# Two small gate loads moved from SyncE's queue to GpSimd's, and four warm-up products taken out

## The chip, the cores and the metric

The kernel runs on one core of a Trainium2 chip. The metric is the device time of one execution in microseconds, as the median of several runs. The profile is that of one execution, and its times count from the start of its span.

## The reference

Block attention whose keys and values are mixed by a normalised 8x8 matrix for each head, followed by a mixture of experts that sends each token to one of eight experts, with a bias by modality:

```
P = sort_net; five times: P = exp(P - rowmax); P /= rowsum; P /= colsum
k_sorted, v_sorted = einsum('bhij,bhjcd->bhicd', P, k_blocks / v_blocks)
attn = softmax(q_block @ k_sorted_block.T / 8);  x = attn @ v_sorted_block      # x: [3072, 512]
logits = x @ w_gate + modality_bias[modality_id];  e = argmax(logits)
out[token] = softmax(logits)[e] * (relu(x @ w1[e]) @ w2[e])
```

Shapes: q, k, v are 4x8x768x64, the sort matrices 4x8x8x8, w_gate 512x8, modality_bias 2x8, w1 8x512x1024, w2 8x1024x512, all float32; modality_id has 3072 entries.

## The kernel before, in words

The 32 (batch, head) pairs are worked in two groups of 16. A group's v (128 rows of 96 blocks' columns x 64) is loaded by four transfers (`load_v`, line 130), its k by three (`load_k`, line 134) and its q by four of 192 KB for each half (`load_q`, line 142). All of these cast float32 to bfloat16 and are issued by GpSimd (POOL), on the software queue. POOL carries out its instructions in the written order, computations and DMA issues in one line; `v_in` is the buffer of v, and is used again for k of the second group.

At the start, VectorE and ScalarE normalise P in five rounds (lines 248 to 281) while TensorE (PE) runs products on the identity whose results nobody reads (`spins`, line 234): ten, ten and eleven inside the rounds, and eight after `make_bd(0)`, which builds the mixing matrix `bd`. Then `sort_v` (line 301) mixes v, and `sort_k` (line 314) mixes k; each chunk of 16 or 64 products is copied out of PSUM by VectorE or ScalarE (lines 95, 97). A product of `sort_v` reads 128 columns of `v_in`, so all four transfers have to be there.

The gate's constants are small: `bias2` (the two bias rows, repeated on 128 partitions, 64 bytes each) and `wg_f` (w_gate, four runs of 32 bytes on each partition). `bias2` is first read by `rank_b` (lines 337 to 343, on POOL), from which `rank_c` (VectorE) derives `eI`, the two experts in use, A and B. `wg_f` is first read by `rank_e` (line 416, on POOL). After `rank_b` the written order of POOL is: `rank_d`, `rank_ok` (small computations), `load_w` for half of expert A's weights (line 430, its address from `eI`), `pads` (memsets, iotas), `load_q` of the second half, `rank_e`, `rank_pen`, `load_w` for the rest of A and all of B, and `load_v` of the second group. Each `load_w` moves 512 KB.

Then come units of attention (`scores`, `expo`, `av`), in which pieces of the experts (`mG` line 534, `mL1` line 566, `mL2` line 580) are run as tokens become ready. From unit 7 on, POOL copies the second group's v into `kv` in four pieces (`relay_v`, line 138), between which it loads the second group's k into the freed parts of `v_in`. After unit 15, PE mixes the second group's v from `kv` (`sort_v(1, ...)`, line 301 again), then k, and runs units 16 to 31 and the rest of the experts. Results leave by indirect DMAs on POOL (line 588).

Of the kernel before, what the change touches and what calls it, by code (L numbers as in the profile page):

```python
# [8 lines left out]
FP32 = mybir.dt.float32  # L9
# [15 lines left out]
def kernel(  # L25
# [13 lines left out]
    nc = tc.nc  # L39
# [5 lines left out]
    E = moe_w_gate.shape[1]  # L45
# [25 lines left out]
    singles = ctx.enter_context(tc.tile_pool(name="singles", bufs=1))  # L71
# [56 lines left out]
    def load_v(g, z, nz=4):  # L128
        cs = slice(z * BLK // nz, (z + 1) * BLK // nz)
        nc.gpsimd.dma_start(out=v_in[:, cs], in_=v_src[g * 128:(g + 1) * 128, cs])  # L130
# [10 lines left out]
    def load_q(g, z, r, hh):  # L141
        nc.gpsimd.dma_start(out=q_in[r][z][:, 4 * hh:4 * hh + 4],  # L142
                            in_=q[2 * g + r, 4 * hh:4 * hh + 4, z * 4 * BLK:(z + 1) * 4 * BLK]
                            .rearrange("h (p t) d -> p h (t d)", t=3))
# [4 lines left out]
    make_identity(nc, ident)  # L149
    load_v(0, 2)  # L150
    load_v(0, 3)

    mod_w = moe_modality_id.tensor.reshape(list(moe_modality_id.tensor.shape)).bitcast(I32).ap()
    modI = singles.tile([32, BLK, 2], I32)
    nc.sync.dma_start(out=modI, in_=bass.AP(tensor=mod_w.tensor, offset=mod_w.offset,
                                            ap=[[2 * BLK, 32], [2, BLK], [1, 2]]))
    bias2 = singles.tile([128, 2, E], FP32)
    nc.sync.dma_start(out=bias2, in_=bass.AP(tensor=moe_modality_bias.tensor, offset=moe_modality_bias.offset,
                                             ap=[[0, 128], [E, 2], [1, E]]))
    wg_f = singles.tile([128, 4, E], FP32)  # L160
    nc.sync.dma_start(out=wg_f, in_=moe_w_gate.rearrange("(c p) e -> p c e", p=128))

    maskUT = singles.tile([128, 128], BF16)
    make_upper_triangular(nc, maskUT, val=1.0, diag=False)
# [34 lines left out]
    for z in range(2):  # L199
        for r in range(2):  # L200
            load_q(0, 0, r, z)
    idI = singles.tile([BLK, 2, 32], I32)
    idm = singles.tile([BLK, 32 * 2 + 128], BF16)
    wgp = singles.tile([128, 2, 5, E + 1], BF16)
# [2 lines left out]
    def pads():  # L207
# [7 lines left out]
        for c in range(5):  # L215
# [7 lines left out]
                     ap=[P_t.ap[0], P_t.ap[2], P_t.ap[1]])  # L223
# [3 lines left out]
                   ap=[ident.ap[0], [1, NB], [NB, 16]])  # L227
# [4 lines left out]
    def spins(n):  # L232
        for _ in range(n):
            nc.tensor.matmul(spin[:, 0].rearrange("p (a b) -> p a b", a=4), ident, id4, start=True, stop=True)  # L234
# [50 lines left out]
    def make_bd(g):  # L285
        rep = ps(f"rep{g}")[:, 0, 0:64].rearrange("p (a b) -> p a b", a=NB)
        nc.tensor.matmul(rep.rearrange("p a b -> p (a b)"), sel[g].rearrange("p a b -> p (a b)"),
                         P_bf.rearrange("p a b -> p (a b)"), start=True, stop=True)
        rtmp = singles.tile([128, NB, NB], FP32, tag="rtmp", name=f"rtmp{g}")
        nc.vector.tensor_tensor(rtmp, rep, bc_mid(jmask, NB), ALU.mult)  # L290
        rr = singles.tile([128, NB], FP32, tag="rr", name=f"rr{g}")
        nc.vector.tensor_reduce(rr, rtmp, AX.X, ALU.add)
        bv = singles.tile([128, 16, NB], BF16, tag=f"bd{g}", name=f"bd{g}")
        (nc.gpsimd if g else nc.vector).tensor_tensor(bv, bmask.broadcast_to([128, 16, NB]), bc_mid(rr, 16), ALU.mult)
        bd.append(bv.rearrange("p a b -> p (a b)"))
# [39 lines left out]
    def rank_b():  # L335
        f_ = st["f"] = small("f_", 1)
        nc.gpsimd.tensor_scalar(f_, cumz[:, 32:33], float(HALF), None, ALU.is_le)
        d_ = small("d_", E)
        nc.gpsimd.tensor_tensor(d_, bias2[:, 1], bias2[:, 0], ALU.subtract)
        bAB = st["bAB"] = singles.tile([128, 2, E], FP32, tag="bAB", name="bAB")  # L340
        nc.gpsimd.tensor_scalar(d_, d_, f_, None, ALU.mult)
        nc.gpsimd.tensor_tensor(bAB[:, 0], bias2[:, 0], d_, ALU.add)
        nc.gpsimd.tensor_tensor(bAB[:, 1], bias2[:, 1], d_, ALU.subtract)
# [280 lines left out]
        return ran  # L624

    make_bd(0)
    spins(8)
    rank_b()
    sort_v(0, 0)
    sort_v(0, 1)  # L630
# [323 lines left out]
```

## Time and profile before

| | |
|---|---|
| median of 3 runs (lowest, highest) | 178.97 us (176.52 to 179.09) |
| the profiled execution: its own time; its span | 177.43 us; 175.8 us |
| PE, DVE, ACT, POOL busy | 158.5 (90%), 99.3 (57%), 96.5 (55%), 78.4 us (45%) |
| software queue (POOL) | 15664 packets, 19.93 MB |
| hardware queue (SyncE) | 768 packets, 0.06 MB |
| TensorE's granted clock, mean | 0.998 |

The span is what the profile shows of the execution; 1.6 us of the execution's own time lie outside of it. Busy time is a share of the whole span, and the stages have different limits, so the table says only that no engine but PE is near its full time; which wait sets the end is read from the rows.

### The profile page before, as it was taken

What the parts mean: (1) busy time and instruction counts of PE and PEld (TensorE: products, weight loads), DVE (VectorE), ACT (ScalarE), POOL (GpSimd) and SP (SyncE); (2) the same over time, 40 slices, a digit from 0 to 9 for tenths busy, and PEclk for the clock granted to TensorE, in tenths of its full rate; (3) what the DMA queues carried; (4) which work ended last, traced back from release to release, by engine and by line L of the source; (5) the groups of instructions that cost most, each with busy time, mean ns of one, the idle gap of its engine ahead of it and who ended that gap; (6) DMA issues with size and microseconds to landing.
All of it is one profiled execution on the core that took longest, in us unless ns stands there. A gap on an engine that the chain in (4) does not pass through costs nothing.

```text
span 175.8 us, 5331 instructions
## 1 busy us (share of the span) xinstructions
PE 158.5 (90%) x2248; PEld 114.9 (65%) x2248; DVE 99.3 (57%) x259; ACT 96.5 (55%) x151; POOL 78.4 (45%) x145
## 2 busy tenths in 40 slices
PE   2998997969999959889899999999999999999970
PEld 0346984758777548768585867867877666775730
DVE  3764966787765593847554667673765632322520
ACT  4212777765766548387556657768567532343220
POOL 7998698782205898982202222002222222242322
PEclk9999999999999999999999999999999999999999
DMA  3999999999999597999410303001100131112211
GB/s 41 154 213 217 197 202 201 122 174 199 207 211 212 137 174 124 172 210 189 101 63 7 117 0 121 4 0 65 60 28 35 63 121 60 60 63 81 98 69 64
DMA packets 16461, 20.37 MB, mean 116 GB/s; under 512 B 9999, under 2 KB 12079, under 8 KB 16432
## 3 DMA queue, kind: packets, MB, share of 16 engines
q0 software_dynamic: 15664, 19.93, 58.4%
q8 instruction: 18, 0.29, 0.7%
q1 hardware_dynamic: 768, 0.06, 0.4%
q14 instruction: 11, 0.09, 0.2%
HBM read 27.32 MB, written 6.55 MB: 193 GB/s over the span
## 4 chain that ended last, share of the span: by engine, by line
PE 54%; POOL 17%; DMA 12%; issue 7%; DVE 6%; POOLq 1%; ACT 0%; DVEq 0%
PE yp L580 19%; PE hp L566 18%; DMA v_in<-in_v_dram 10%; PE spin L234 6%; POOL kv L138 6%; DMA q_in<-in_q_dram 3%; POOL q_in L142 3%; PE ka L314 2%; PE sc L448 2%; PE op L468 2%; POOL out_dram L588 2%; PE lg L534 1%; DVE y L587 1%; DVE xb L473 1%; PE tq L324 1%
## 5 line engine op out<-in xcount | busy, mean ns | idle before, releaser
L588 POOL DMA_INDIRECT out_dram<-y,ids x25 | 25.1, 1002 | 76.7 <-ACT y L585 34.1
L580 PEld LDWEIGHTS <-hT 128*128 128x128 bf16 x200 | 18.3, 98 | 19.2
L454 ACT ACTIVATE attnT<-sc 96x768 bf16<-96x768 f32 x32 | 25.5, 806 | 9.4 <-PE sc L448 9.3
L554 ACT ACTIVATE hT<-hp 128x512 bf16<-128x512 f32 x37 | 21.8, 595 | 11.0 <-PE hp L566 8.5
L566 PE MATMUL hp<-XT,wB 128*128 128x256 bf16 (+1 forms) x224 | 24.9, 265 | 0.1
L580 PE MATMUL yp<-wB,hT 128*128 128x512 bf16 x104 | 24.3, 379 | 0.0
L587 DVE TENSOR_SCALAR y<-yp,gate 128x512 f32<-128x512 f32 x13 | 9.8, 750 | 24.2 <-PE yp L580 24.2
L566 PE MATMUL hp<-XT,wA 128*128 128x128 bf16 (+1 forms) x256 | 23.1, 246 | 0.3 <-DVE xb L473 0.2
L580 PE MATMUL yp<-wA,hT 128*128 128x512 bf16 x96 | 22.7, 380 | 0.0
L473 DVE TENSOR_TENSOR xb<-op,rs_all 96x512 bf16<-96x512 f32 x32 | 22.0, 687 | 1.1
L566 PEld LDWEIGHTS <-wB 128*128 128x128 bf16 x224 | 19.9, 98 | 3.0 <-DVE xb L473 0.2
L566 PEld LDWEIGHTS <-wA 128*128 128x128 bf16 x256 | 19.3, 97 | 2.1 <-DVE xb L473 0.4
L585 ACT ACTIVATE y<-yp,gate 128x512 f32<-128x512 f32 x12 | 8.3, 688 | 15.0 <-PE yp L580 15.0
L509 DVE CAST XT<-pm 128x720 f32 x16 | 14.5, 908 | 1.9 <-PE pm L499 0.8
L468 PEld LDWEIGHTS <-attnT 96*128 96x128 bf16 x256 | 11.8, 97 | 4.6 <-DVE xb L473 0.9
L472 DVE RECIPROCAL rs_all<-op 96x8 f32<-96x8 f32 x32 | 6.4, 199 | 14.0 <-PE op L468 13.7
L95 ACT CAST v_sb<-va 96x1024 bf16<-96x1024 f32 x11 | 10.7, 1012 | 6.5 <-PE va L301 6.4
L509 ACT CAST XT<-pm 128x720 f32 x16 | 12.3, 769 | 3.5 <-PE pm L499 2.1
L138 POOL COPY kv<-v_in 128x1536 bf16<-128x1536 bf16 x4 | 11.3, 2842 | 6.5 <-DMA v_in<-in_v_dram 6.5
L234 PE MATMUL spin<-ident 128*128 128x512 bf16 x39 | 11.1, 444 | 3.3 <-POOL ident masks.py:199 3.3
L468 PE MATMUL op<-v_sb,attnT 96*128 96x65 bf16 x256 | 13.0, 193 | 1.0 <-DVE xb L473 0.7
L555 DVE TENSOR_SCALAR hT<-hp 128x512 bf16<-128x512 f32 x13 | 8.9, 688 | 7.2 <-PE hp L566 7.1
(157 smaller groups left out, 222.9 us busy)
## 6 DMA issues: line engine op xcount, KB each, us to landing
v_in<-in_v_dram POOLq DMA_DIRECT2D x8, 384.0 KB, 13.7
q_in<-in_q_dram POOLq DMA_DIRECT2D x16, 192.0 KB, 7.4
wA<-in_moe_w_dram POOLq DMA_DIRECT2D x4, 512.0 KB, 8.1
wB<-in_moe_w_dram POOLq DMA_DIRECT2D x4, 512.0 KB, 12.9
kv<-in_k_dram POOLq DMA_DIRECT2D x3, 512.0 KB, 13.7
v_in<-in_k_dram POOLq DMA_DIRECT2D x3, 512.0 KB, 6.3
out_dram<-y,ids POOLq DMA_INDIRECT x25, 2.7
modI<-in_moe_modality_id_dram SPq DMA_DIRECT2D x1, 24.0 KB, 1.6
```

The lines of the kernel that those rows point to most:

```text
L95: nc.scalar.copy(dst, src)
L138: nc.gpsimd.tensor_copy(kv[:, 0:BLK * D].rearrange("p (d c) -> p d c", c=BLK)[:, :, cs], v_in[:, cs].rearrange("p c d -> p d c"))
L234: nc.tensor.matmul(spin[:, 0].rearrange("p (a b) -> p a b", a=4), ident, id4, start=True, stop=True)
L454: nc.scalar.activation(attnT[u % 2][:, 0:8 * BLK].rearrange("p (r f) -> p r f", r=2), sc_tiles.pop(u)[0:BLK, :, 0:4 * BLK], ACT.Exp, scale ...
L468: nc.tensor.matmul(op[:, r, j * (D + 1):(j + 1) * (D + 1)], attnT[u % 2][:, c0:c0 + 128], v_sb[0:BLK, r * 64 + (hh * 4 + j) * 8 + i, 0:D + ...
L473: nc.vector.tensor_tensor(xb[t % XB][:, :, hh * 256:(hh + 1) * 256].rearrange("p r (j d) -> p r j d", j=4), o4[:, :, :, 0:D], rs_all[:, u] ...
L509: ins = (nc.scalar.copy if side(t) == "act" else nc.vector.tensor_copy)(d, s_).ins
L554: return nc.scalar.activation(dst, src, ACT.Relu)
L566: mm = nc.tensor.matmul(hp[:, f], w1_t[m][:, c, fc * 128:(fc + 1) * 128], XT[:, c, row:row + n], start=(c == 0), stop=(c == 3))
L580: nc.tensor.matmul(yp, hT[s % 2][:, f, z * 128:(z + 1) * 128], w2_t[m][:, f], start=(f == 0), stop=(f == 7))
L587: nc.vector.tensor_scalar(y, yp, g_, None, ALU.mult)
L588: ins = nc.gpsimd.indirect_dma_start(out=out, out_offset=bass.IndirectOffsetOnAxis(ap=ids[:, k_:k_ + 1], axis=0), in_=y, in_offset=None, b ...
```

## The change

`bias2` is loaded by POOL right after the four transfers of v, and `wg_f` by POOL right after the four of the first half of q, where SyncE loaded both, third and fourth of its queue. The run of warm-up products behind `make_bd(0)` has four in place of eight. Nothing else differs; what is computed is the same.

```diff
     load_v(0, 2)
     load_v(0, 3)
+    bias2 = singles.tile([128, 2, E], FP32)
+    nc.gpsimd.dma_start(out=bias2, in_=bass.AP(tensor=moe_modality_bias.tensor, offset=moe_modality_bias.offset,
+                                               ap=[[0, 128], [E, 2], [1, E]]))
 
     mod_w = moe_modality_id.tensor.reshape(list(moe_modality_id.tensor.shape)).bitcast(I32).ap()
     modI = singles.tile([32, BLK, 2], I32)
     nc.sync.dma_start(out=modI, in_=bass.AP(tensor=mod_w.tensor, offset=mod_w.offset,
                                             ap=[[2 * BLK, 32], [2, BLK], [1, 2]]))
-    bias2 = singles.tile([128, 2, E], FP32)
-    nc.sync.dma_start(out=bias2, in_=bass.AP(tensor=moe_modality_bias.tensor, offset=moe_modality_bias.offset,
-                                             ap=[[0, 128], [E, 2], [1, E]]))
     wg_f = singles.tile([128, 4, E], FP32)
-    nc.sync.dma_start(out=wg_f, in_=moe_w_gate.rearrange("(c p) e -> p c e", p=128))
...
     for z in range(2):
         for r in range(2):
             load_q(0, 0, r, z)
+    nc.gpsimd.dma_start(out=wg_f, in_=moe_w_gate.rearrange("(c p) e -> p c e", p=128))
...
     make_bd(0)
-    spins(8)
+    spins(4)
     rank_b()
     sort_v(0, 0)
```

## Rows read from the trace of the kernel before

**Rows 1.** The page: busy tenths of PE in 40 slices of 4.4 us.

```profile
PE   2998997969999959889899999999999999999970
```

**Rows 2.** The chain that ended last, in order of time (start us, us).

```profile
37.62 16.82 DMA v_in<-in_v_dram
54.50 2.22 POOL kv L138
...
66.05 2.87 POOL kv L138
```

**Rows 3.** All engines in order of time, 65 to 81 us (start us, us).

```profile
69.23 1.23 PE L301 MATMUL va<-bd,kv 128*128 128x128 bf16 x16
```

**Rows 4.** POOL in order of time, first 38 us.

```profile
3.21 1.08 POOL L130 DMA_DIRECT2D v_in<-in_v_dram  x2
...
12.76 0.74 POOL L142 DMA_DIRECT2D q_in<-in_q_dram  x1 [0.29 <-DMA v_in<-in_v_dram]
13.58 0.25 POOL L337 TENSOR_SCALAR f__274<-cumz 128x1 f32<-128x1 f32 x1
...
14.79 0.21 POOL L343 TENSOR_TENSOR bAB<-bias,d__276 128x8 f32<-128x8 f32 x1
...
20.69 1.55 POOL L430 DMA_DIRECT2D wA<-in_moe_w_dram  x2 [1.23 <-issue]
...
24.83 3.02 POOL L142 DMA_DIRECT2D q_in<-in_q_dram  x4
...
32.97 1.59 POOL L430 DMA_DIRECT2D wA<-in_moe_w_dram  x2 [0.38 <-issue]
```

**Rows 5.** DMA in 40 slices, 28 to 38 us: GB/s.

```profile
GB/s 180 246 168 189 202 181 205 180 192 188 189 184 194 194 191 183 194 194 250 129 81 68 60 55 25 25 79 57 25 106 147 115 156 193 188 164 205 201 209 201
```

**Rows 6.** Line 130, landing of the v loads of 3.2 and 3.8 us.

```profile
DMA to landing us min/median/max: 9.3/9.3/9.3
...
DMA to landing us min/median/max: 9.3/9.9/10.6
```

**Rows 7.** All engines in order of time, 37 to 80 us.

```profile
39.22 0.54 POOL L130 DMA_DIRECT2D v_in<-in_v_dram  x1 [0.50 <-DMA wA<-in_moe_w_dram]
...
42.73 0.53 POOL L130 DMA_DIRECT2D v_in<-in_v_dram  x1 [2.97 <-DMA wA<-in_moe_w_dram]
...
48.41 1.91 PE L566 MATMUL hp<-XT,wB 128*128 128x256 bf16 x16
```

**Rows 8.** Line 430, landing: wA issued at 33.0, 33.8; wB at 34.8, 35.4.

```profile
DMA to landing us min/median/max: 6.0/7.3/8.6
...
DMA to landing us min/median/max: 10.2/11.1/12.0
```

**Rows 9.** DMA queues and issues, first 20 us (last column: us to landing).

```profile
q1 hardware_dynamic: 768, 0.06, 3.6%
...
wg_f<-in_moe_w_gate_dram SPq DMA_DIRECT2D x1, 16.0 KB, 9.5
```

**Rows 10.** PE in order of time, first 40 us.

```profile
3.32 4.45 PE L234 MATMUL spin<-ident 128*128 128x512 bf16 x10 [3.32 <-POOL ident masks.py:199]
...
12.70 1.90 PE L234 MATMUL spin<-ident 128*128 128x512 bf16 x8
14.47 1.63 PE L301 MATMUL va<-bd,v_in 128*128 128x128 bf16 x16
16.83 1.20 PE L314 MATMUL ka<-bd,kv 64*64 64x64 bf16 x64 [0.73 <-DMA kv<-in_k_dram]
...
39.06 0.48 PE L463 MATMUL op<-ident 128*128 128x252 bf16 x3 [1.27 <-ACT attnT L454]
```

**Rows 11.** SyncE's queue in order of time.

```profile
2.24 0.43 SPq L161 DMA_DIRECT2D wg_f<-in_moe_w_gate_dram  x1
```

**Rows 12.** DVE in order of time, first 40 us.

```profile
13.32 0.29 DVE L294 TENSOR_TENSOR bd<-bmask,rr 128x128 bf16<-128x128 f32 x1
...
17.28 0.15 DVE L347 TENSOR_REDUCE mxb<-bAB 128x2 f32<-128x16 f32 x1
```

## The prediction

> **What bounds the kernel now.** I read the slices of the page first: from the sixteenth on PE is busy for eight tenths or more in all but the last two [rows 1], so PE carries the second half, and what counts is when that half may begin. The chain of waits answers that: it runs through the landing of the second group's v at 54.44, the four copies of `relay_v` on POOL, the last of which ends at 66.05 + 2.87 = 68.92, and the first `sort_v` product of the second group [rows 2, 3]. That product starts at 69.23, with no wait shown on PE: PE arrived just then. The copies are early by some 0.25 us, no more.
>
> Going back from 54.44, the queue is full and in order, up to a hole: the rate falls from about 190 to 25 GB/s between 32.8 and 35.3 and then stays near 200 [rows 5]. What fills it again is the second half of expert A, issued by POOL at 32.97 [rows 4]; flow returns 1.5 to 2.3 us after that issue began. POOL had no stop between 12.76 and 32.97 that another engine ended: it computes, issues, computes; its 1.23 us before 20.69 are its own register work ("issue") [rows 4]. So **a microsecond added to POOL before 32.97 reaches the end**, less the 0.25 us.
>
> One wait of POOL matters for this change. The fourth q load stood 0.29 us for a transfer of v [rows 4]; the third v load had landed at 3.21 + 9.3 = 12.51 [rows 6]. Much later the third and fourth loads of the second v stood 0.50 and 2.97 us for wA [rows 7]; those landed at 33.0 + 6.0 = 39.0 and 33.8 + 8.6 = 42.4 [rows 8]. Count the software queue's transfers in written order: the 11th waits for the 3rd, the 26th for the 18th, the 27th for the 19th. Each waits for the one eight before; eight are in flight at most, and POOL stands still until there is room. (A limit on packets wouldn't fit: by the tiles' shapes 2,688 would be open in the first case, while the 25th transfer went through with 2,816.) SyncE's transfers don't enter this count.
>
> **The change part by part.**
>
> *Off SyncE's queue.* That queue's 768 packets take 3.6% of 16 engines over 20 us, 11.5 engine-us or 15 ns each [rows 9]; bias (128) and gate weights (512) are 640 of these, 0.60 us of every engine. They were in the way of v: wg_f was issued at 2.24 and landed 9.5 us later [rows 9, 11], ahead of the fourth v at 3.76 + 10.6 = 14.36 [rows 6]. The fourth v can come sooner by 0 (if the small packets fell into gaps) to 0.60; I take 0.5, since most of them ran beside a filled queue: **13.86**. SyncE's freed time serves nobody.
>
> *Four products fewer.* Eight took 1.90 us [rows 10], four end near 13.7; `bd` is ready at 13.61 [rows 12]. But in the profile `sort_v` starts at 14.47, right behind the landing of the fourth v, not behind the products. The cut alone is worth nothing to 0.1 us; with v earlier the start moves to about 13.9, 0.55 us sooner. PE is idle there for 0.2 us, or 0.8 if v doesn't come sooner. The products at the start show the lower level, 4.45 us for ten, and half of that later; after a gap of 1.27 us PE still ran at the upper one [rows 10] while the granted clock was 0.998 over the span. I charge nothing. The Trainium skill ("TensorE: Matmul & The Clock Gate", HAM oscillation) warns that a wait for data between products can drop the clock; that speaks against this part, and is a rival below.
>
> *Bias on POOL.* One more issue between v and k: as a v load of as many pieces, two of which took 1.08 [rows 4]; 0.55. It shifts k and the q loads. No cost by itself: v keeps the transfer engines busy until 13.86, and k was issued long before.
>
> *Gate weights on POOL.* One more issue behind the fourth q: 512 pieces like a q load, 0.74 to 0.76 us [rows 4]; 0.75.
>
> *The new waits.* With one more transfer in front, the fourth q is the 12th and waits for the 4th, the last v, instead of the third; the gate weights are the 13th and wait for the 5th, the bias. Before: landing 12.51, issue at 12.76, so 0.25 us to react. After: 13.86 + 0.25 = 14.11, q to 14.85, gate weights to 15.60. The bias, 0.12 us of packets behind v, has landed by then: no wait of its own. `rank_b` starts at 15.68, where it was at 13.58: **POOL is 2.1 us late**. Behind it stand `rank_c`, which VectorE began at 17.28 [rows 12] behind a v copy (`rank_b` took 1.42 us to 15.00 [rows 4], so its result now comes at 17.1: no stop), `load_w`, the second q, `rank_e`, and all later loads. wA's first half is issued at 22.8, into a queue that still holds q; its second half at 35.1. The hole grows by 2.1 us. The later pairs of the eight-in-flight rule keep their partners, both moved by two.
>
> A rule against this: the Trainium skill ("SBUF — State Buffer", SBUF: two separate sides) says that some VectorE copies lock GpSimd out, so that descriptors of its transfers can't be written, while SyncE's aren't touched. By that, the gate weights' issue could be held for one VectorE copy, an estimate of 1.2 us more. In this trace four q issues took 3.02 us beside VectorE's copies, 0.755 each, against 0.74 for the one alone [rows 4]: I add nothing.
>
> *Sum.* The last `relay_v` ends at 68.92 + 2.1 = 71.0. Does PE get there later still? Its weights land 2.1 later too: wB's first two at 35.4 + 12.0 + 2.1 = 49.5 [rows 8], where PE wanted them at 48.41 [rows 7] or sooner: 1.1 late, below 2.1, so the relays decide and the 0.55 us of the start is lost in them. End: 2.1 − 0.25 = 1.85, **+1.8 us**. Span 177.6, time 177.43 + 1.8 = 179.2 on the profiled execution's scale. The median of the runs is 1.54 higher, on its scale 180.8; the three runs spread over 2.6 us, and I predict the middle, **180.0**.
>
> Bounds: POOL's delay is 1.0 at least (0.55 + 0.75, less the 0.29 no longer waited: all issues, no new wait), and 3.8 at most (the bias landing only with the first k, at 16.8 less 0.5 [rows 10], then 0.25, 0.75 and 0.08 to 17.4). That is +0.75 to +3.6 us; less than nothing is excluded for POOL, since two issues are added to an engine that never rests there.
>
> **The rivals.** The times stand on the same middle scale, 178.2 plus the change. (1) *No new wait*: the limit of eight counts otherwise. POOL is 1.0 late: +0.75, 179.0. For it: three cases only. Against: they fit without remainder.
>
> (2) *The bias lands late*: small writes with a full k queue behind them report only when the slowest engine is through, at worst with the first k. Place: POOL's issue of the gate weights. It decides as soon as the bias lands after 14.6, one for one. At 16.3, +3.6 us: 181.8, slower by 2.0%. For it: wg_f took 9.5 us on its own queue [rows 9]. Against: that was beside v, and here 8 packets an engine stand behind v in order.
>
> (3) *The hole swallows the delay*: if the second q's tail, not the issue at 32.97, set the restart at 35.3, up to 1.7 us are free and the end is the same, 178.3. For it: rate was not zero in the hole [rows 5]. Against: at 25 GB/s most transfer engines had nothing left to do, and full rate came only after the new issue. More than this can't be won: the relays can't be earlier than POOL, so the 0.55 us at the start has no way to the end.
>
> (4) *The clock drops* in the gap before `sort_v`: the lower level lasted 4.45 us at the start and cost half of it, 2.2; PE would reach `sort_v(1)` later than the relays: +2.2, 180.4. The Trainium skill's page on the clock gate, named above, has this rule. Against: a 1.27 us gap without it.
>
> (5) *The change doesn't do what it says*: v doesn't come sooner. Then POOL is 2.6 late and the end +2.3, 180.5.
>
> **How the numbers follow.** Forecast 0.50, (5) 0.13, (1) 0.13, (2) 0.11, (3) 0.10, (4) 0.03. What a measurement of this kernel can tell from no change is about 2%, 3.6 us. Only (2), and (5) with a late bias, pass that: slower 0.14; faster 0.03 for what I don't see; the same 0.83. The range runs from 177.7 to 182.4: the hole case and the upper bound, each with some 0.6 us for the runs' own spread.
>
> **What would show it.** Right: the fourth q issue waits until the fourth v lands, near 14.1; gate weights issued near 14.9; `rank_b` near 15.7; wA's second half near 35.1; the hole longer by 2 us; the second v landing near 56.5; PE waiting before its first `va` of the second group, near 71. Wrong: `rank_b` before 14.7 (1), after 16.5 (2); a second v landing within 0.5 us of 54.44 (3); PE reaching `sort_v(1)` after POOL's last copy by over 0.5 us, which would make PE's own path the limit.

## The result and the profile after

| | before | after |
|---|---|---|
| median (lowest, highest) of 20 runs | 178.75 us (176.52 to 180.92) | 179.66 us (178.4 to 181.29) |
| the profiled execution: its own time; its span | 177.43; 175.8 us | 178.64; 177.0 us |
| TensorE's granted clock in it, mean | 0.998 | 0.981 |

Ratio 1.0066, 95% interval 1.0040 to 1.0091: 0.0066 of 178.75 is **+1.2 us**, the same as the difference of the two profiled spans; the medians differ by 0.9. Here and below medians are of all runs, while a ratio leaves out runs over 1.5% above the fastest of their kernel.

POOL in order of time, after (start us, us, what; in brackets the idle time before and who ended it):

```profile
3.21 1.09 POOL L130 DMA_DIRECT2D v_in<-in_v_dram  x2
4.28 0.56 POOL L153 DMA_DIRECT2D bias<-n_moe_modality_bias_dram  x1
...
10.72 3.02 POOL L142 DMA_DIRECT2D q_in<-in_q_dram  x4
14.60 0.76 POOL L201 DMA_DIRECT2D wg_f<-in_moe_w_gate_dram  x1 [0.85 <-DMA bias<-n_moe_modality_bias_dram]
15.43 0.24 POOL L337 TENSOR_SCALAR f__270<-cumz 128x1 f32<-128x1 f32 x1
...
34.78 1.60 POOL L430 DMA_DIRECT2D wA<-in_moe_w_dram  x2 [0.39 <-issue]
...
43.95 0.53 POOL L130 DMA_DIRECT2D v_in<-in_v_dram  x1 [2.73 <-DMA wA<-in_moe_w_dram]
```

The four q loads now go out without a stop; the wait stands one place later, before the gate weights, and it is for the bias. `rank_b` starts at 15.43 instead of 13.58 and wA's second half is issued at 34.78 instead of 32.97 [rows 4]: POOL is 1.85 and then 1.81 us late. The landings explain the two halves of this. Line 130's loads of 3.2 and 3.8 us, after:

```profile
DMA to landing us min/median/max: 6.9/7.7/8.5
```

So the third v is there at 3.21 + 6.9 = 10.1 and the fourth at 3.76 + 8.5 = 12.3, where they came at 12.51 and 14.36 [rows 6]. But the bias, issued half a microsecond behind the last v, is late. DMA in 40 slices over 0 to 20 us, and two of the issue lines (KB each, us to landing), after:

```profile
GB/s 0 0 0 10 42 63 80 104 135 203 191 184 203 221 215 203 203 209 215 215 227 218 124 68 92 107 156 164 213 213 213 205 213 221 213 205 221 221 181 192
...
bias<-n_moe_modality_bias_dram POOLq DMA_DIRECT2D x1, 8.0 KB, 10.0
wg_f<-in_moe_w_gate_dram POOLq DMA_DIRECT2D x1, 16.0 KB, 11.6
```

4.28 + 10.0 is 14.3, **two microseconds behind v**, and at just that place, from 11 to 14 us, the rate falls from about 215 to 68 GB/s and comes back. The six slices moved 355 KB where 3 us at 215 would have moved 645: 290 KB, or 1.35 us of the full rate, are lost. The first k, queued behind, lands no sooner than before (5.56 + 11.4 = 16.96, where it was 5.00 + 11.8 = 16.8), though v is through two microseconds earlier. PE in order of time, after:

```profile
12.52 1.04 PE L234 MATMUL spin<-ident 128*128 128x512 bf16 x4
13.48 1.59 PE L301 MATMUL va<-bd,v_in 128*128 128x128 bf16 x16
17.02 1.92 PE L314 MATMUL ka<-bd,kv 64*64 64x64 bf16 x64 [1.95 <-DMA kv<-in_k_dram]
...
69.75 0.41 PE L468 MATMUL op<-v_sb,attnT 96*128 96x65 bf16 x8
70.43 1.07 PE L301 MATMUL va<-bd,kv 128*128 128x128 bf16 x16 [0.28 <-POOL kv L138]
```

`sort_v` starts a microsecond sooner than before (14.47 [rows 10]) and PE then stands 1.95 us for k, where it stood 0.73; that first chunk of 64 products takes 1.92 us. The last line is where the end is decided: PE now waits 0.28 us for POOL's last copy, where it came just after it [rows 3]. The chain that ended last, after, shows what released it:

```profile
39.42 16.49 DMA v_in<-in_v_dram
55.97 2.02 POOL kv L138
...
67.55 2.84 POOL kv L138
70.43 1.08 PE va L301 x16
```

The second v lands at 55.9 (+1.47), the last copy ends at 67.55 + 2.84 = 70.39 (+1.47), and `va` starts 1.20 later than the 69.23 of before, which is the whole difference of the spans. That it comes out so exactly is in part luck: both executions take 106.57 us from there to their ends (175.8 − 69.23, 177.0 − 70.43), but the profiled execution of e1 below, at a granted clock of 0.995, takes 108.1 (177.2 − 69.09). Between the landing and POOL's lateness lies the hole of [rows 5]. DMA in 40 slices, 30 to 40 us, after:

```profile
GB/s 109 136 101 105 123 135 141 161 166 216 167 169 177 183 183 189 186 183 160 100 84 60 40 23 12 52 70 36 115 176 201 217 184 197 209 201 205 188 184 107
```

From the first slice under 130 GB/s to the next over 100 it lasts from 34.75 to 37.0 (32.75 to 35.25 before): it has moved by about two microseconds with wA's issue, and has not grown.

### The profile page after: what moved, and what is told of

It reads as the page before. It is cut to its first block, busy times and chain, and to the rows that moved or that the text cites. A ratio compares the mean times of both kernels' runs of the same rounds, so it can differ in the third digit from the quotient of the medians.

```text
span 177.0 us, 5323 instructions
## 1 busy us (share of the span) xinstructions
PE 157.5 (89%) x2244; PEld 115.2 (65%) x2244; DVE 99.6 (56%) x259; ACT 96.3 (54%) x151; POOL 80.5 (45%) x147
## 4 chain that ended last, share of the span: by engine, by line
PE 49%; POOL 18%; DVE 11%; DMA 9%; issue 7%; ACT 2%; POOLq 1%; DVEq 0%
PE yp L580 20%; PE hp L566 18%; DMA v_in<-in_v_dram 9%; POOL kv L138 6%; DVE XT L509 2%; PE ka L314 2%; PE sc L448 2%; POOL q_in L142 2%; DVE y L587 2%; PE op L468 2%; PE va L301 1%; PE lg L534 1%; DVE xb L473 1%; PE tq L324 1%; POOL out_dram L588 1%
## 5 line engine op out<-in xcount | busy, mean ns | idle before, releaser
L468 PEld LDWEIGHTS <-attnT 96*128 96x128 bf16 x256 | 11.8, 97 | 4.6 <-DVE xb L473 0.9
L95 ACT CAST v_sb<-va 96x1024 bf16<-96x1024 f32 x11 | 10.7, 1013 | 6.4 <-PE va L301 6.4
L509 ACT CAST XT<-pm 128x720 f32 x16 | 12.3, 768 | 3.1 <-PE pm L499 2.1
L234 PE MATMUL spin<-ident 128*128 128x512 bf16 x35 | 9.6, 430 | 3.3 <-POOL ident masks.py:199 3.3
```

The costliest lines, as they stand in the source:

```text
L95: nc.scalar.copy(dst, src)
L468: nc.tensor.matmul(op[:, r, j * (D + 1):(j + 1) * (D + 1)], attnT[u % 2][:, c0:c0 + 128], v_sb[0:BLK, r * 64 + (hh * 4 + j) * 8 + i, 0:D + ...
L509: ins = (nc.scalar.copy if side(t) == "act" else nc.vector.tensor_copy)(d, s_).ins
```

## The experiments

Each ratio is to the kernel before, on the same chip; e1 to e4 ran on one chip, e5 to e8 on a second, e9 to e12 on a third.

**Which part costs.** Three kernels do one part alone, and one undoes one part.

*e1_products*, the shorter warm-up alone:

```diff
-    spins(8)
+    spins(4)
     rank_b()
```

> The kernel before with four warm-up products in place of eight, nothing else. Theory: the first value product waits for the fourth v transfer, not for the products, so it still starts near 14.4 us, the time is that of before within 0.2 us, and the granted clock stays at the upper level across a gap of some 0.8 us. Rival: the longer gap lowers the clock; products at 1.2 GHz then show behind 14.4 us and the end moves by 0.5 us or more.

Measured: 179.61 us beside 179.76, ratio 0.9989 (0.9953 to 1.0024). PE waited 0.64 us for the fourth v before `va` at 14.56. The products cover a wait for v and nothing else.

*e2_bias*, the bias alone, placed as in the change:

```diff
     load_v(0, 3)
+    bias2 = singles.tile([128, 2, E], FP32)
+    nc.gpsimd.dma_start(out=bias2, in_=bass.AP(tensor=moe_modality_bias.tensor, offset=moe_modality_bias.offset,
+                                               ap=[[0, 128], [E, 2], [1, E]]))
```

> The kernel before with the bias alone moved to POOL behind v; gate weights on SyncE, eight products. Theory A (small packets cost v in proportion to their number, and the gate weights are most of them): the fourth v lands near 14.2, the fourth q issue waits for it, rank_b starts near 15.3 and the end is 1.0 to 1.3 us later. Theory B (the bias's 128 packets, all read from the same 64 bytes, are the expensive ones): the fourth v lands near 12.5, the transfer engines show a hole behind it, rank_b's first read of the bias waits to about 14.5, POOL is 0.3 to 0.6 us late and the end moves by 0.3 us at most.

Measured: 180.12 beside 179.76, ratio 1.0014 (0.9982 to 1.0046). POOL in order of time:

```profile
13.42 0.74 POOL L142 DMA_DIRECT2D q_in<-in_q_dram  x1 [0.41 <-DMA v_in<-in_v_dram]
...
15.45 0.21 POOL L339 TENSOR_TENSOR d__276<-bias 128x8 f32<-128x8 f32 x1 [0.97 <-DMA bias<-n_moe_modality_bias_dram]
...
34.61 1.59 POOL L430 DMA_DIRECT2D wA<-in_moe_w_dram  x2 [0.38 <-issue]
```

Without the gate weights, the first reader of the bias waits for it, 0.97 us, and POOL ends up 1.64 late at wA's second half, where 0.3 to 0.6 was expected. The late bias alone makes most of POOL's delay. The time of all runs hardly shows it; it shows when they are sorted by clock, at the end of this section.

*e3_gate*, the gate weights alone, as in the change (the SyncE load goes, the line below comes behind the first four `load_q`):

```diff
+    nc.gpsimd.dma_start(out=wg_f, in_=moe_w_gate.rearrange("(c p) e -> p c e", p=128))
```

> The kernel before with the gate weights alone moved to POOL behind the first q; bias on SyncE, eight products. Theory A: the fourth v lands near 13.9, the gate weights' issue waits for it, rank_b starts near 15.0 and the end is some 0.9 us later. Theory B: the fourth v still lands near 14.3, rank_b starts near 15.4, and the end is 1.0 to 1.3 us later, as much as the whole change.

Measured: 179.13 beside 179.76, ratio 0.9958 (0.9926 to 0.9991). The gate weights are then the 12th transfer, and POOL stood 0.40 us for v before issuing them at 13.58; wA's second half went out at 33.83, 0.86 late, and the last copy ended at 66.66 + 2.82 = 69.48, 0.56 late. Both theories had the end 0.9 us or more later, and both are wrong: this part alone costs nothing, and may gain.

*e4_eight*, the change with `spins(8)` kept:

> The changed kernel with eight warm-up products again. The first value product then starts near 14.4 in place of 13.5, and the idle time before the first k product falls from 1.95 to about 1 us. Theory (POOL's relays set the end): the clock no longer falls to 0.50 behind 17 us, PE runs up to 0.9 us earlier between 20 and 66 us, and the end is that of the change within 0.3 us, since PE only waits longer for the relays. Rival (the clock's fall is what made the change slow): the end goes back by 0.7 us or more towards the kernel before.

Measured: 180.96 beside 179.76, ratio 1.0035 (0.9999 to 1.0071). POOL waits for the bias as in the change (0.87 us, gate weights at 14.63). PE, busy with the products until 14.46, stands 0.88 us for the first k and runs its chunk in 1.20 us, not 1.92. The interval overlaps that of the change, so a gain of time by four products more isn't shown. By the clock, 5 of these 12 runs have a mean granted clock of 0.986 or less, much as in the kernel before (13 of 35 on this chip); of the change's 20 runs, on another chip, 16 have.

**POOL's lateness or the clock.** The change has two things that could make it slow: POOL 1.85 us late, and a spell of half clock after the wait for k. PE in windows, after (us from and to, length, busy (instructions), granted clock, DMA share, GB/s):

```profile
15.00:17.00 2.00, 0.07 (x1) 0.89 1.06 213
17.00:19.00 2.00, 1.98 (x65) 0.50 1.07 215
19.00:21.00 2.00, 1.65 (x16) 0.75 1.28 197
21.00:24.00 3.00, 2.93 (x92) 1.00 1.45 173
```

*e5_filler* delays POOL and leaves the loads and the products as before; the tile is read by nobody. Behind the first `load_q`:

```diff
+    fill = singles.tile([128, 1024], U32)
+    for _ in range(2):
+        nc.gpsimd.memset(fill, 0)
```

> The kernel before with two memsets of a tile that nobody reads (0.95 us each) on POOL between the first q loads and rank_b; all loads where they were. POOL is then 1.9 us late as in the change, while v, k and PE's first stage are as before. Theory P (POOL's lateness reaches the end through the second v and the relays): the last relay ends 1.5 us later and runs with a full clock are 1.1 to 1.4 us longer. Theory C (the change is slower only because the clock falls in the gap before the first k product): no difference, within 0.4 us.

Measured: 180.19 beside 179.06, ratio 1.0091 (1.0047 to 1.0135). The memsets took 2.04 us; at wA's first half POOL was 1.66 late, at the second, issued at 33.96, only 0.99. The last copy ended at 66.88 + 2.84 = 69.72, 0.80 late. Delay on POOL alone makes this kernel slower. It cost more than the sum has for it (0.80 less the slack): in this profile PE came to `va` at 70.63, 0.9 us after the copy. The granted clock shows what held PE; in the same windows it was 1.00 in the kernel before:

```profile
60.00:66.00 6.00, 4.02 (x63) 0.88 0.68 122
66.00:72.00 6.00, 5.92 (x73) 0.84 0.79 137
```

*e6_warm*, the change, with the wait for k filled by products behind `sort_v(0, 1)`:

```diff
     sort_v(0, 1)
+    spins(8)
     rank_c()
```

> The changed kernel with eight warm-up products more, between the second value chunk and the first k chunk, where PE stood idle for 1.95 us. POOL is as late as in the change. Theory C: the spell of half clock at 17 us is gone in most runs, and the median falls back to that of before within 0.4 us. Theory P: the spell is gone too, but the median stays 0.8 us or more over before, since the relays still come 1.5 us late.

Measured: 181.08 beside 179.06, ratio 1.0141 (1.0083 to 1.0198). PE in the first two windows:

```profile
15.00:17.00 2.00, 1.89 (x17) 1.00 1.06 213
17.00:19.00 2.00, 2.00 (x75) 1.00 1.07 217
```

The clock stays at its upper level there, the first k chunk takes 1.20 us at 16.87, POOL's last copy still ends at 67.50 + 2.83 = 70.33, and the kernel is no faster. The half clock after the wait is real, and the slowness doesn't need it. (This execution, 182.97 us, is the longest of the six; its clock falls later, to 0.78 over 66 to 72 us.)

*e7_gate_later*, only the gate weights moved, to behind `rank_ok()` and before the first `load_w` (bias on SyncE, eight products):

```diff
     rank_ok()
+    nc.gpsimd.dma_start(out=wg_f, in_=moe_w_gate.rearrange("(c p) e -> p c e", p=128))
     for z in range(2):
```

> The kernel with only the gate weights moved, issued later: on POOL right before the first load of expert A, behind rank_ok; bias on SyncE, eight products. rank_b no longer stands behind a wait for v: it starts near 13.3, expert A's second half is issued near 33.4, 0.4 us later than before. v and k land about 1 us earlier than before, as with the gate weights alone. Theory P: end 0.1 us later than before at most, and earlier than the gate weights alone by 0.2 us. If PE's own path sets the end: 0.5 to 1.0 us earlier than before.

Measured: 179.08 beside 179.06, ratio 0.9996 (0.9948 to 1.0043); wA's second half at 32.80, the last copy ended at 68.67 and `va` started at 69.80, with a granted clock of 0.82 over 66 to 72 us. The forecast gain of PE's own path doesn't show in the ratio; it does among runs of a like clock, below.

*e8_no_hole*, e7 with two computations of POOL moved behind the rest of A's weights, so that the queue isn't left empty:

```diff
-    rank_e()
-    rank_pen()
     for z in range(2, 4):
         load_w("A", z)
+    rank_e()
+    rank_pen()
```

> The kernel of the run before this one, and rank_e and rank_pen moved behind the loads of expert A's second half, so that these are issued some 5 us earlier and the hole in the queue between 33 and 35 us closes. The second v lands near 52.5 in place of 54.4 and the relays end near 67. Theory P: the relays stop setting the end; then it is 0.5 to 1.2 us earlier than before, held by PE's own path. If PE's own path sets the end already: no gain over the run before this one.

Measured: 177.75 beside 179.06, ratio 0.9964 (0.9923 to 1.0005). DMA in 40 slices, 28 to 44 us, then POOL and PE in order of time:

```profile
GB/s 205 215 173 196 191 186 194 185 190 191 225 180 186 199 206 206 204 205 207 207 205 202 210 210 205 220 205 253 200 200 215 195 215 215 205 220 205 202 213 189
...
63.49 2.82 POOL L138 COPY kv<-v_in 128x1536 bf16<-128x1536 bf16 x1
...
69.10 1.23 PE L300 MATMUL va<-bd,kv 128*128 128x128 bf16 x16
```

The hole of [rows 5] is gone and the last copy ends at 66.31, 2.6 us sooner than before; `va` starts at 69.10, only 0.13 sooner, at a granted clock of 1.00 up to there. **At the upper clock PE's own way ends near 69 even when POOL is early**: in the kernel before, the two arrive together. In such an execution delay on POOL costs almost at once, and a gain on POOL brings almost nothing before `va`.

**What is wrong with the bias.** It is a transfer of 8 KB, and it costs the queue 290 KB. In the change's trace its packets on POOL's queue are 16 of 512 B. This is how long they took, beside the same transfer in two more kernels:

```
change, first profile   40 ns x5, then 220, 248, 266, 342, 996, 1268, 1508, 1795, 1807, 1841, 1898
e10_change              40 ns x5, then 145, 164, 167, 800, 1192, 1478, 1556, 1801, 1806, 1912, 1949
e2_bias                 40 ns x8, then 145, 202, 249, 371, 532, 1572, 1693, 1751
```

All 128 pieces of this transfer are read from the same 64 bytes. The gate weights' 16 packets of 1,024 B, from 512 different places, took 59 ns each. So the theory: it is the one source address, not the size and not the extra transfer. The Trainium skill ("DMA: Bandwidth & Descriptors", Specifications) puts the line below which small transfers lose rate at 512 B; as packets of 512 B these should run well by that, and the 40 ns ones did. No run here bears out a size as the cause.

*e11_rows* tests it: the change, with the bias back on SyncE's queue (third, as before) and in its place on POOL a load of the same shape and piece size that nobody reads, from 128 different rows.

```diff
-    nc.gpsimd.dma_start(out=bias2, in_=bass.AP(tensor=moe_modality_bias.tensor, offset=moe_modality_bias.offset,
-                                               ap=[[0, 128], [E, 2], [1, E]]))
+    rows2 = singles.tile([128, 2, E], FP32)
+    nc.gpsimd.dma_start(out=rows2, in_=bass.AP(tensor=moe_w_gate.tensor, offset=moe_w_gate.offset,
+                                               ap=[[2 * E, 128], [E, 2], [1, E]]))
```

> The changed kernel with the bias back on SyncE and, in its place on POOL's queue, a load of the same shape (128 partitions, 64 bytes each) that reads 128 different rows and that nobody uses. If the bias's late landing comes from 128 reads of the same 64 bytes, the hole in the transfer rate behind v (to 70 to 110 GB/s around 12 us) is gone, this transfer's packets take 40 ns each, the first k lands 1 us earlier and the gate weights' issue no longer waits 0.85 us. If small pieces as such are the cause, the hole stays, with single packets of 1.3 to 1.9 us.

Measured: 179.01 beside 179.59, ratio 0.9996 (0.9959 to 1.0034). All 16 packets took 40 ns. DMA over 0 to 20 us, then POOL, then PE:

```profile
GB/s 0 0 0 10 41 71 49 88 138 113 125 119 132 112 185 203 209 197 233 203 227 209 197 209 227 236 197 229 221 197 213 221 205 229 189 238 221 197 238 148
...
13.32 0.74 POOL L142 DMA_DIRECT2D q_in<-in_q_dram  x1 [0.32 <-DMA v_in<-in_v_dram]
14.06 0.76 POOL L204 DMA_DIRECT2D wg_f<-in_moe_w_gate_dram  x1
...
15.58 1.20 PE L317 MATMUL ka<-bd,kv 64*64 64x64 bf16 x64 [0.51 <-DMA kv<-in_k_dram]
...
68.58 0.41 PE L471 MATMUL op<-v_sb,attnT 96*128 96x65 bf16 x8
69.57 1.07 PE L304 MATMUL va<-bd,kv 128*128 128x128 bf16 x16 [0.58 <-POOL kv L138]
```

There is no hole at 11 to 14 us, the first k product starts 1.4 us sooner than in the change (1.35 us of rate were lost there), and the gate weights go out without a wait. From 4.5 to 7 us the queue runs at 112 to 132 GB/s, while SyncE's bias is under way (issued at 1.76, landed 5.9 later), against 184 to 221 in the change: on SyncE's queue, too, v runs slower beside this small load. PE is 0.4 sooner than before by its line before `va` (68.58 against 68.99), and stands 0.58 us for POOL, whose two more issues make the last copy 0.6 late.

*e10_change* is the change itself on that chip.

> The changed kernel itself, on the same chip as the next two, so that its runs can be sorted by granted clock beside runs of before. Theory P (POOL's lateness sets the end): among runs of full clock it is 0.8 to 1.3 us longer than before. Theory C (the clock's fall): runs of full clock are equal, and the change only has more spells of half clock.

Measured: 181.05 beside 179.59, ratio 1.0127 (1.0075 to 1.0180). POOL waited 1.47 us for the bias, PE 2.68 us for the first k, and the last copy ended at 71.06:

```profile
15.24 0.76 POOL L201 DMA_DIRECT2D wg_f<-in_moe_w_gate_dram  x1 [1.47 <-DMA bias<-n_moe_modality_bias_dram]
...
17.72 1.92 PE L314 MATMUL ka<-bd,kv 64*64 64x64 bf16 x64 [2.68 <-DMA kv<-in_k_dram]
```

None of the six runs had the full clock (0.965 to 0.979, where only 3 of the 23 of before lie), so the comparison that was planned couldn't be made. e11 has the same issues on POOL and the same products: the source of that one load, with the bias back on SyncE's queue, makes 2 us of the medians, the clock's part included. **The source of that load is the cause of the hole, of the wait for the bias and of the late k.** That it is the repetition of one address is the likely reading, but e11 also reads another tensor: a load that reads the bias's tensor without repeating it, or repeats one row of another, wasn't run.

*e9_before* is one more profile of the kernel before, on that chip.

> The kernel before itself, for a second profile on the chip of the next three. If the fourth v's landing is the same in every execution, the first k product starts at 16.8 as in the first profile. If it varies (two of the experiments that left SyncE's loads where they were show 15.7 and 16.9), it can start near 15.7 here; what the experiments showed of PE's first stage has then to be read against both.

Measured: 180.59 in this one run, beside 179.59. Its PE in windows, then POOL and PE in order of time:

```profile
40.00:50.00 10.00, 10.00 (x163) 0.83 1.16 201
60.00:72.00 12.00, 9.82 (x124) 0.86 0.77 130
...
65.81 2.83 POOL L138 COPY kv<-v_in 128x1536 bf16<-128x1536 bf16 x1
...
72.66 1.21 PE L301 MATMUL va<-bd,kv 128*128 128x128 bf16 x16
```

POOL's last copy ended at 68.64 (68.92 in the first profile), and PE came to `va` at 72.66, where 69.23 stands in [rows 3]: with PE busy throughout 40 to 50 us the granted clock was 0.83 there, 1.00 in the first profile. By these rows four microseconds of lateness on POOL would have cost this execution nothing, so a cost of POOL's path can show only in some of the runs. The first k product started at 16.88, as in the first profile, where e5, with the same loads, has 15.70: this differs between executions.

*e12_cut*, the best of what was seen: e8 and `spins(4)`.

> The kernel without the hole (gate weights later on POOL, rank_e and rank_pen behind expert A's second half, bias on SyncE) with four warm-up products in place of eight. The relays have 2.6 us to spare there, so PE's own path sets the end. If v has landed by 13.9 and k by 15.2, PE starts 0.5 to 0.9 us earlier and the end comes 0.4 to 0.8 us earlier than with eight products, 1.2% below before. If PE then waits for k instead, nothing is won, and a spell of half clock may cost 0.8 us.

Measured: 178.37 beside 179.59, ratio **0.9949** (0.9916 to 0.9982). The last copy ended at 63.27 + 2.78 = 66.05, and the first k product started at 15.60 after a wait of 0.29. This version beats both kernels, by 0.9 us against the one before, less than the 1.2% expected. In its profile, its longest run, `va` starts only at 71.11, at a granted clock of 0.71 over 66 to 72 us. That four products help here isn't shown: the interval overlaps e8's.

**The runs sorted by clock.** Each run's mean granted clock is on record. The table takes only runs with 0.994 or more (with 0.992 or 0.996 in its place every sign that can be formed is the same but e1's), beside those of the kernel before on the same chip, and the profile's last copy against the 68.92 of before.

| | last copy, us late | median of such runs (of all) | before (of all) | us |
|---|---|---|---|---|
| e4, bias and gate weights | 1.80 | 179.67 (3 of 12) | 178.63 (8 of 35) | +1.0 |
| e2, bias | 1.42 | 179.69 (5 of 12) | 178.63 | +1.1 |
| e6, the change and products | 1.41 | 179.47 (1 of 6) | 178.44 (12 of 28) | +1.0 |
| e5, POOL delayed | 0.80 | 179.16 (3 of 11) | 178.44 | +0.7 |
| e11, other source | 0.60 | 178.23 (4 of 10) | 178.48 (9 of 23) | −0.25 |
| e3, gate weights | 0.56 | 178.10 (6 of 12) | 178.63 | −0.5 |
| e1, products | −0.02 | 178.82 (4 of 12) | 178.63 | +0.2 |
| e7, gate weights later | −0.25 | 177.53 (6 of 12) | 178.44 | −0.9 |
| e8, no hole | −2.61 | 177.46 (5 of 12) | 178.44 | −1.0 |
| e12, no hole, four products | −2.87 | 177.31 (2 of 12) | 178.48 | −1.2 |

At such clocks each of the three kernels with the bias on POOL's queue is about a microsecond slower, e2 too, and e5, which delays POOL alone, 0.7: POOL's lateness costs without the clock's fall. Where the gate weights left SyncE's queue and the bias stayed, the time is shorter, even with a last copy 0.6 late. That gain isn't seen at `va` in e8, and its place wasn't traced. The clock costs as well: 16 of the change's 20 runs are at 0.986 or less, with a median of 179.92, and its four others have one of 178.58; the clocks of the 20 runs of before beside them are not on record.

## Why the prediction was right, and where its sum was off

The forecast was +1.8 us in the middle of runs, to 180.0; it came to +1.2, at 179.66. That 180.0 and 179.66 lie so close is partly luck: the forecast counted from 178.2, while 20 runs of the kernel before have a median of 178.75. The way was the forecast one: POOL late at wA's second half, the queue late behind it, PE waiting for the last copy. The first step of the sum had two terms wrong, an early v and a late bias, which partly cancelled; that POOL's delay came out near 2.1 is luck to that extent.

**Eight in flight: right.** The gate weights, 13th, waited for the 5th; in e3, as 12th, for the 4th; in e2 and e11 the fourth q, 12th, waited for the fourth v. The later pairs kept their partners: the fourth load of the second v stood 2.73 us for wA, landed at 35.62 + 8.0 = 43.6, and went out at 43.95.

**The fourth v sooner by 0.5, at most 0.60: wrong.** It came 2.06 us sooner. The step that failed is 15 ns a packet, taken from busy time: SyncE's packets cost v more than the time they are shown busy. With the bias alone put back (e11) the fourth v lands at 3.76 + 9.3 = 13.06, so the bias makes 0.76 of it. The other 1.3 isn't shown to be the gate weights': in e5, with both loads where they were, the fourth v landed at 3.75 + 9.3 = 13.05, against 3.74 + 10.7 = 14.44 in e1. Line 130's loads, the fourth in e5, then the third and fourth in e11:

```profile
DMA to landing us min/median/max: 9.3/9.3/9.3
...
DMA to landing us min/median/max: 8.0/8.6/9.3
```

The prediction took one execution's 14.36 for the kernel's. As v was early, the fourth q, whose issue was due at 12.98, found it landed and didn't wait.

**"The bias has landed by then: no wait of its own": wrong, and the cause of the wait.** It was priced at 0.12 us of packets behind v; it landed 2.0 behind. Rival (2) had the right place, the issue of the gate weights, and a wrong reason: not a full queue behind the bias, since e11's load of the same shape in the same place makes no wait, but the bias's source.

**POOL 2.1 late: 1.85.** Issues 0.56 + 0.76, wait 0.85, less the 0.29 no longer waited: 1.88.

**The hole grows by 2.1: it moved instead,** and the delay was passed on: 1.81 at the issue of wA, 1.47 at the second v's landing; the queue gave back 0.34, which is rival (3) in a small part. `va` began 0.31 behind the last copy before and 0.04 after, which leaves 1.47 − 0.27 = 1.20. Of the 0.65 by which the forecast's 1.85 was too much, 0.29 are POOL's (2.1 for 1.81), 0.34 the queue's and 0.02 the slack.

**Four products fewer: nothing, right** (e1). With v early and k late they leave PE a gap that the prediction didn't look for: it looked before `sort_v`, rival (4), and the gap came behind it, before k. There the granted clock did fall to 0.50, the lower level of 1.2 GHz, after 1.95 us without work. The Trainium skill ("TensorE: Matmul & The Clock Gate", HAM oscillation), which the prediction weighed, describes a clock that falls in longer waits for data; this trace shows the fall behind a shorter one. So does e10, where the chunk took 1.92 us after 2.68 us; in e2 the chunk after a wait of 2.10 us took 1.20 and only the next 1.92. In the change's profile PE's own way was 0.76 late (69.75 against 68.99), less than POOL's 1.47, as the prediction had it of PE's way, though for another reason: wB wasn't waited for (49.17, 0.76 late like all before it).

**Open.** How much of the 1.2 us is the copies and how much the clock: e4 and e2 put the late bias at about 1 us without the clock, but on another chip, and the gate weights' gain stands against it. Where that gain comes from. Whether the repetition or the tensor makes the bias's reads slow. And whether the bias would do harm on POOL's queue at a later place, which wasn't tried.

## What to carry to other kernels

Where an engine issues its loads in written order, count the transfers in flight, here eight at most: a load costs its issue, and may cost a wait for a transfer eight places before it that has nothing to do with it. Here 8 KB, a few bytes repeated on all partitions, held a queue as long as 290 KB would have; put such a load where nobody is queued behind it. Where two paths reach the same point together, a delay of one costs there, and neither can gain there alone. Where the clock varies from run to run, sort the runs by it before a cost is called hidden or shown.

## What the hardware showed that I had not expected

- 128 reads of the same 64 bytes, in 16 packets of 512 B, took up to 1.95 us a packet, with 40 ns for others of the same transfer and 40 ns for all of a load of 128 different rows of another tensor. On SyncE's queue the bias is 128 packets of 8 to 24 ns each.
- The Trainium skill ("DMA: Bandwidth & Descriptors", Issuing engine by pattern) gives simple loads to SyncE as the generally faster way. For the gate weights e3 measured nothing lost on POOL's queue (0.9958, 0.9926 to 0.9991), where they are 16 packets of 59 ns instead of 512 small ones. For the bias the runs agree with it.
